# Attention and two expert layers on one core: where three steps of the hand-over to the second expert layer stand in the program

## The chip, the cores and the metric

The kernel runs on one core of a Trainium2 chip, with TensorE (PE), VectorE (DVE), ScalarE (ACT), GpSimd (POOL), SyncE (SP, which here issues DMAs) and the DMA engines. The metric is the device time of one execution in microseconds, as the median of several runs.

## The reference

What is computed, cut to what matters here (4 batches, 8 heads, 576 positions, 64 per head; 2304 tokens of 512; 8 experts with an inner width of 1024):

```python
scores = scale * q @ k.T                       # plus log-decay from f, causal mask
x = softmax(scores) @ v                        # attention; heads side by side: 2304 x 512

def expert_layer(x, logits, w1, w2):           # run twice, with its own weights
    expert_idx = argmax(logits, axis=1)        # one expert for a token
    gate_w = softmax(logits)[range(N), expert_idx]
    for e in range(8):
        mask = expert_idx == e
        h = maximum(x[mask] @ w1[e], 0)        # w1[e]: 512 x 1024
        out[mask] = gate_w[mask, None] * (h @ w2[e])   # w2[e]: 1024 x 512
# layer 1: logits = normed(x) @ normed(expert_emb).T / tau
# layer 2: logits = x @ w_gate, x being what layer 1 gave
```

## The kernel before, in words

The program is one long list of instructions for each engine, in an order written out by hand: each engine works down its list and waits on semaphores where data of another engine is needed. Matrices are kept as a high and a low part, so every product is three matmuls (high by high, high by low, low by high), all recorded at line 1169.

**An expert.** The tokens of one expert are gathered as rows of a DRAM table (`gather`, line 512: an indirect DMA that POOL issues, one for each 128 tokens), turned into columns on PE (`xtrans`, line 520) and split into parts `xh` on ACT (line 523) and `xl` on DVE (line 524). Then come eight W1 steps (`w1_step`, m = 0 to 7, 12 matmuls each; ACT writes `hh`, line 1186, DVE writes `hl`, line 1187) and four W2 groups (`w2_step`, d = 0 to 3, 24 matmuls each for up to 512 tokens, PSUM into `yt`). Weights arrive as chunks `raw` of 512 KB through four buffers; a split (`wts.splits_to`: ACT line 482, DVE line 483) makes the two parts `w`, and the load of a later chunk waits for the split that frees its buffer. A layer takes its experts by rank, fullest first; rank r of layer 1 has room for `CAPS1[r]` tokens, here 256 for the last three, rank 0 of layer 2 for 560.

**The routing of layer 2** is worked out while layer 1 ends. For each finished expert of layer 1 a chain of small links follows: `hot` (which expert a token wants: six DVE instructions, lines 217 to 223), `places` (counts on PE, lines 229 to 253), `leading` (line 323 and on: which expert of layer 2 will be rank 0; from here its weights may be loaded), `slots` (seven DVE instructions, lines 268 to 284, with one each on ACT, line 280, and POOL, line 281), `sums` (matmuls at line 295 and an addition at line 303), and for the last but one expert also `rows` (the index list `idxl2e`, lines 338 to 414, and two gathers of the first 256 tokens of layer 2's rank 0 into `rows`) and `early_columns_2` (those rows into columns `x0h`, `x0l`).

For the last but one expert the string `LATE` says behind which step of the last expert a link stands: a letter and a number, 0 to 7 a W1 step, 8 to 11 a W2 group (h hot, p places, l leading, s slots, u sums, r rows, c early columns).

**The hand-over.** The string `TURN2` then lists what stands between the two layers. The letters: `L` routing products of the last expert's tokens (16 matmuls of 8 columns, line 1269), `R` its output rows (8 transposes, line 1299, and stores to the table), `H`, `P`, `S` its hot, places and sums, `G` the index list `idxl` and three gathers `xg`, the rest of rank 0; `m`k the W1 step k of layer 2's rank 0 on its first 256 tokens and `e`k its ACT and DVE part; `w68` a split; `x`t turns gathered tile t (2, 3, 4) into columns. `I` is `general_1`: a branch (line 1577) around the code for tokens that found no room; with these inputs the branch is taken and its body, hundreds of instructions on PE, is jumped over. `O` is `order_2`: ten DVE instructions (lines 348 to 420) that put the other seven experts of layer 2 in order and give the index list `idxb` of their tokens.

`L2.run` goes on from there. It first gathers the rank 1 tokens (from `idxb`), then does the rest of rank 0's W1 steps, on tokens 256 to 559, 304 columns (called m0' to m7' in this text), then W2; the columns of rank 1 are made behind the first W2 group.

Of the kernel before, what the change touches and what calls it, by code (L numbers as in the profile page):

```python
# [19 lines left out]
P = 128  # L20
NE = 8
# [13 lines left out]
RAWS, RING, LOOK = 4, 6, 4  # L35
FIRST, EARLY = 1, 256
TURN1 = "w2 w3 m0 m1 P e0 m2 e1 w4 m3 S e2 G m4 e3 m5 e4 O m6 e5 x2 m7 e6 e7"
LATE = "h4 p5 l5 s7 u8 r8 c11"
TURN2 = "L R m0 H P e0 m1 m2 e1 S G m4 w68 m3 m6 m5 e3 e2 e6 e4 x2 e5 x3 m7 e7 x4 I O"

PRO = (
# [29 lines left out]
def kernel(  # L71
# [16 lines left out]
    B, H, S, D = q.shape  # L88
# [51 lines left out]
    capr = [const.tile([P, NE], F32, name=f"capr{i}") for i in range(2)]  # L140
# [193 lines left out]
    def pick_lead(sp, acc, fb, Q, name):  # L334
# [6 lines left out]
        )  # L341
        nc.vector.tensor_reduce(ids, x, axis=AX.X, op=ALU.add)
        return ids
# [159 lines left out]
    wts = Weights(wr, wp)  # L503
# [23 lines left out]
    with ExitStack() as actx:  # L527
        p3 = actx.enter_context(tc.tile_pool(name="a3", bufs=3))
# [389 lines left out]
        tots, keys = {-1: None}, {}  # L918
# [180 lines left out]
    class Layer:  # L1099
        def __init__(self, first, pools, weights, src, caps, base):  # L1100
            self.first, self.wts, self.src, self.caps, self.base = first, weights, src, caps, base
            self.sp, self.xp, self.hp, self.yp, self.pp, self.pt, self.pq = pools
            self.cw = P if first else YC
            self.lo = KC * self.cw
            self.w0 = 0 if first else 64
            self.xg, self.nm, self.gt, self.scatters, self.h0, self.x, self.early, self.late = {}, {}, {}, [], None, None, {}, []

        def gather(self, t, ids):
            g = self.xp.tile([P, XW2], F32, tag="xg", name="xg")
# [240 lines left out]
        def early_again(self):  # L1350
            for t in list(self.late):
                self.lead_columns(t)
            for m in list(self.early):
                self.early_mm(m)
                self.early_relu(m)

        def lead_rows(self, idx):

            self.xg[0] = rows0 + [self.gather(t, idx[:, t : t + 1]) for t in range(len(rows0), self.tiles(0))]

        def run(self, idx, idf, pad, after_rank, side):
            caps, wts, w0 = self.caps, self.wts, self.w0
            self.idx, self.idf, self.pad = idx, idf, pad
            yt = None
            for r in range(NE):
                C, b = caps[r], w0 + r * 8
                if r + 1 < NE:
                    self.start_gather(r + 1)
                later = {}
                Hh = self.new_h() if r else self.h0  # L1370
                spans = self.spans(C)
                if r == 0:
                    X = self.x
                    for m in range(FC):
                        self.w1_step(m, wts.ws[b + m // 2], slice(EARLY, C), X, Hh)
                        if m == 2:
                            self.nm[0] = self.norms(self.xg[0])
                        if m == 5:
                            self.start_gates(0)
                        if m % 2:  # L1380
                            wts.splits_to(b + RING - 2 + m // 2)
                else:
                    for m in range(FC):
                        wts.splits_to(min(b + m // 2 + LOOK, w0 + 64))
                        for sl in spans:
                            self.w1_step(m, wts.ws[b + m // 2], sl, X, Hh)
                        if 1 <= m <= self.tiles(r - 1):
                            self.out_step(r - 1, yt, m - 1)
                            if m == self.tiles(r - 1):
                                later = after_rank(r - 1)  # L1390
                        for fn in later.get(m, ()):
                            fn()
                        if self.first and m == 5:
                            self.start_gates(r)
                if not self.first and r == NE - 1:
                    wts.splits_to(w0 + 64)
                    self.last_rows(r, [wts.ws[b + 4 + c] for c in range(4)], Hh)
                    break
                yt = self.new_y()
                for d in range(KC):  # L1400
                    wts.splits_to(min(b + 4 + d + LOOK, w0 + 64 + 4 * self.first))
                    self.w2_step(d, wts.ws[b + 4 + d], C, Hh, yt)
                    for fn in later.get(FC + d, ()):
                        fn()
                    next(side, None)
                    if r + 1 < NE:
                        nt = self.tiles(r + 1)
                        if d == 0:
                            X = self.new_x()
                        for t in [[(0,), (1,), (2,), ()], [(0,), (1, 2), (3, 4), ()]][nt > 3][d]:  # L1410
                            if t < nt:
                                self.xtrans(t, self.xg[r + 1], caps[r + 1], X)
                        if d == 1:
                            self.nm[r + 1] = self.norms(self.xg[r + 1])
                            if not self.first:
                                self.start_gates(r + 1)
            self.yt = yt
# [55 lines left out]
    with ExitStack() as mctx:  # L1473
        sp = mctx.enter_context(tc.tile_pool(name="sp", bufs=1))
# [10 lines left out]
        key2 = sp.tile([P, NE], F32, name="key2")  # L1485
# [3 lines left out]
        def after1(r):  # L1489
# [32 lines left out]
            todo = {}  # L1522
            for u in (LATE if r == NE - 2 else "h4 p6 s7 u10").split():
                todo.setdefault(int(u[1:]), []).append(steps[u[0]])
# [19 lines left out]
        L1 = Layer(True, pools, wts, x_dram, CAPS1, BASE1)  # L1544
        L2 = Layer(False, pools, wts, y_dram, CAPS2, BASE2)
        got = {}
# [16 lines left out]
            TURN1,  # L1563
        )
        (idx1, idf1), pad1, (_, hot1) = got["idx"], got["pad"], got["hot"]
        L1.run(idx1, idf1, pad1, after1, general(sp, keys[B - 1], hot1, capr[0], True))


        last = after1(NE - 1)
# [5 lines left out]
        def general_1():  # L1575
            bg, cap, ci, anew = gen[True]
            with tc.If(nv1 > 0):  # L1577
                go = general_tokens(sp, oh1, pos1, cap, T1)
                ids = assign(sp, pq, "pl", T1, go, pos1, bg, tp1f, "g")
                idxg, idfg = to_index(sp, ids, NC1, N, "g")  # L1580
                padg = to_pad(sp, ids, idfg, NC1, "g")
                kept = [wts.raws[i] for i in range(wts.nsplit, wts.nsplit + RAWS)]
                L1.loop(ci, idxg, idfg, padg, kept, L2.x, x0, L2.h0)
                pm = sp.tile([P, 24], F32, name="pm")
                nc.vector.tensor_tensor(pm, pad1, capmask, op=ALU.max)
                nc.vector.tensor_scalar(pm, pm, anew, None, op0=ALU.add)
                nc.vector.tensor_tensor(padg[:, 0:24], padg[:, 0:24], pm, op=ALU.min)
                route_a(rp, logit2, padg, oh2, NC1)
                route_b(pq, "pl", oh2, pos2, None, NC1, "g", key2)
                for t in range(0, NC1, 5):  # L1590
                    cols = slice(t, min(t + 5, NC1))
                    n = cols.stop - t
                    hots = place_a(rp, pos2[:, cols, :], oh2[:, cols, :], tp2[:, cols], n, Q2)
                    place_b(pq, "pl", *hots, n, Q2, acc2, t == 0, "g")
                nc.vector.tensor_copy(got["l2"], lead_index("l3"))
                L2.early_rows(got["l2"], NC1 * P)
                for t in range(len(rows0), L2.tiles(0)):
                    gather_rows(y_dram, L2.xg[0][t], got["l2"][:, t : t + 1])
                for i, raw in enumerate(kept):
                    wts.load_chunk(wts.nsplit + i, raw)  # L1600
                early_columns_2()
                L2.early_again()

        def order_2():
            sig2, hot2 = got["hot"] = order(sp, key2, lead2[0][1])
            wts.known(1, sig2, range(1, NE))
            ids = by_rank(sp, acc2, hot2, Q2)
            got["idx"] = to_index(sp, ids, 8 * Q2, NC1 * P, "b")
            got["pad"] = to_pad(sp, ids, got["idx"][1], 8 * Q2, "b")
# [4 lines left out]
            {  # L1614
                "m": L2.early_mm, "e": L2.early_relu, "x": L2.lead_columns, "L": lambda: L1.last_logits(L1.yt, NE - 1), "H": last[0],
                "R": lambda: L1.out_last(NE - 1, L1.yt), "P": last[1], "S": last[2], "G": lead_index_2,
                "I": general_1, "O": order_2,
            },
            TURN2,
        )  # L1620
        (idx2, idf2), pad2, (_, hot2) = got["idx"], got["pad"], got["hot"]
        L2.run(idx2, idf2, pad2, lambda r: {}, general(sp, key2, hot2, capr[1], False))
        bg, cap, ci, _ = gen[False]
        nv2 = L2.tile_count(ci)
        with tc.If(nv2 > 0):
# [35 lines left out]
```

## Time and profile before

| | |
|---|---|
| median of 3 runs | 825.51 us (818.5 to 826.73) |
| the profiled execution: own time | 827.05 us |
| its span, first to last instruction | 825.3 us |
| PE busy (matmul) | 778.5 us, 94% |
| PE weight load busy | 739.0 us, 90% |
| DVE, ACT, POOL busy | 545.7, 474.1, 237.2 us |
| mean granted TensorE clock | 0.967 |

Times inside the profile count from the start of the span. Attention ends and layer 1 begins near 270 us; the hand-over to layer 2 lies between some 531 and 592 us. A busy PE is not PE at its peak: at the lower of its two clocks it is as busy and does half.

### The profile page before, as it was taken

What the parts mean: (1) busy time and instruction counts of PE and PEld (TensorE: products, weight loads), DVE (VectorE), ACT (ScalarE), POOL (GpSimd) and SP (SyncE); (2) the same over time, 40 slices, a digit from 0 to 9 for tenths busy, and PEclk for the clock granted to TensorE, in tenths of its full rate; (3) what the DMA queues carried; (4) which work ended last, traced back from release to release, by engine and by line L of the source; (5) the groups of instructions that cost most, each with busy time, mean ns of one, the idle gap of its engine ahead of it and who ended that gap; (6) DMA issues with size and microseconds to landing.
All of it is one profiled execution on the core that took longest, in us unless ns stands there. A gap on an engine that the chain in (4) does not pass through costs nothing. (4 is left out here: it accounts for less than half of the span.)

```text
span 825.3 us, 16797 instructions
## 1 busy us (share of the span) xinstructions
PE 778.5 (94%) x5863; PEld 739.0 (90%) x5863; DVE 545.7 (66%) x1510; ACT 474.1 (57%) x1095; POOL 237.2 (29%) x450
## 2 busy tenths in 40 slices
PE   5999999999999889999999999978899999999995
PEld 4788888988988889999999999968899999999994
DVE  3688887888888834767666777754464556666661
ACT  4788777777778425464565565533343455565650
POOL 5653443543524330321311320112121230122000
PEclk9999999999999957999999999988899999999998
DMA  5858756556663324636646656562244456668740
GB/s 129 203 134 229 187 142 175 138 139 152 164 184 94 98 78 128 202 107 192 195 145 188 193 166 193 162 195 97 83 154 142 151 184 198 197 214 236 205 139 15
DMA packets 201261, 130.51 MB, mean 158 GB/s; under 512 B 85098, under 2 KB 188522, under 8 KB 201167
## 3 DMA queue, kind: packets, MB, share of 16 engines
q1 hardware_dynamic: 195439, 112.47, 48.2%
q0 software_dynamic: 5200, 16.83, 6.1%
q8 instruction: 51, 0.84, 0.4%
q14 instruction: 43, 0.35, 0.1%
q10 hardware_dynamic: 528, 0.02, 0.0%
HBM read 112.05 MB, written 17.75 MB: 157 GB/s over the span
## 5 line engine op out<-in xcount | busy, mean ns | idle before, releaser
L1169 PE MATMUL ps<-xh,w 128*128 128x256 f32 (+8 forms) x1024 | 226.5, 308 | 3.5 <-PEq L1577 2.2
L1169 PE MATMUL ps<-hh,w 128*128 128x256 f32 (+7 forms) x1024 | 218.8, 301 | 0.0
L483 DVE TENSOR_TENSOR w<-raw,w 128x1024 fp32r<-128x1024 f32 x124 | 151.5, 1224 | 56.4 <-ACT w L482 55.8
L1169 PEld LDWEIGHTS ps<-xh,w 128*128 128x128 f32 x1024 | 176.6, 199 | 5.0 <-issue 4.5
L1169 PEld LDWEIGHTS ps<-hh,w 128*128 128x128 f32 x1024 | 168.7, 189 | 1.1 <-ACT hh L1186 0.2
L1169 PE MATMUL ps<-xl,w 128*128 128x256 f32 (+8 forms) x512 | 155.7, 304 | 0.0
L1169 PE MATMUL ps<-hl,w 128*128 128x256 f32 (+7 forms) x512 | 153.1, 299 | 1.4 <-DVE hl L1187 1.3
L1186 ACT ACTIVATE hh<-ps 128x256 fp32r<-128x256 f32 (+8 forms) x144 | 56.1, 397 | 148.8 <-PE ps L1169 146.2
L482 ACT ACTIVATE w<-raw 128x1024 fp32r<-128x1024 f32 x128 | 132.9, 1053 | 0.0
L1187 DVE SCALAR_TENSOR_TENSOR hl<-ps,hh 128x256 fp32r<-128x256 f32 (+8 forms) x144 | 62.8, 441 | 62.7 <-ACT hh L1186 61.5
L1169 PEld LDWEIGHTS ps<-xl,w 128*128 128x128 f32 x512 | 101.9, 199 | 0.2
L1169 PEld LDWEIGHTS ps<-hl,w 128*128 128x128 f32 x512 | 96.9, 189 | 2.9 <-DVE hl L1187 2.5
L745 DVE CUSTOM_DVE_ANT_0 sp<-pS,cum 128x512 f32<-128x512 f32 (+3 forms) x128 | 61.1, 486 | 26.9 <-PE pS L738 25.4
L756 ACT ACTIVATE pm<-sp,sm 128x512 f32<-128x512 f32 (+3 forms) x128 | 71.2, 558 | 4.4 <-DVE sm L745 3.2
L1237 POOL DMA_INDIRECT out_dram<-y,tok x23 | 23.1, 1005 | 175.4 <-ACT y L1233 138.7
L820 DVE TENSOR_TENSOR ptl<-pT,pth 128x128 fp32r<-128x128 f32 (+3 forms) x128 | 59.7, 486 | 9.6 <-ACT pth L817 9.5
L817 ACT ACTIVATE pth<-pT 128x128 fp32r<-128x128 f32 (+3 forms) x128 | 53.6, 435 | 10.6 <-PE pT L813 9.3
L813 PE MATMUL pT<-ident,pm 128*128 128x128 f32 x320 | 57.4, 280 | 1.6 <-DVE ptl L820 1.1
L855 PE MATMUL po<-pth,vv 128*128 128x128 f32 (+2 forms) x192 | 55.9, 310 | 0.1
L855 PE MATMUL po<-ptl,vv 128*128 128x128 f32 (+2 forms) x192 | 53.4, 312 | 0.0
L281 POOL TENSOR_TENSOR l_R<-l_R,tp 128x120 bf16<-128x120 bf16 (+1 forms) x12 | 7.4, 616 | 157.7 <-DVE l_R L276 142.5
L680 POOL CAST qn<-q 128x256 fp32r<-128x256 f32 (+1 forms) x62 | 19.5, 314 | 87.2 <-PE pq L693 54.9
(312 smaller groups left out, 1464.5 us busy)
## 6 DMA issues: line engine op xcount, KB each, us to landing
raw<-in_moe_w_dram SPq DMA_DIRECT2D x128, 512.0 KB, 4.3
cum<-cum_dram SPq DMA_DIRECT2D x15, 576.0 KB, 5.2
k<-in_k_dram SPq DMA_DIRECT2D x64, 128.0 KB, 2.8
cumt<-cum_dram SPq DMA_DIRECT2D x32, 144.0 KB, 4.6
y_dram<-y SPq DMA_DIRECT2D x16, 276.5 KB, 3.6
q<-in_q_dram SPq DMA_DIRECT2D x32, 128.0 KB, 2.5
v<-in_v_dram SPq DMA_DIRECT2D x32, 128.0 KB, 3.2
x_dram<-x SPq DMA_DIRECT2D x16, 256.0 KB, 2.4
```

The source lines that it names most:

```text
L482: nc.scalar.activation(hi, raw, AF.Copy)
L483: eng.tensor_tensor(lo, raw, hi.bitcast(F32), op=ALU.subtract)
L745: nc.vector.tensor_tensor_reduce(out=sp[:, :w], in0=st[j, s, "S", i][:, :w], in1=cums[j][0][:, s, :w], scale=1.0, scalar=3.0e38, op0=ALU.a ...
L756: nc.scalar.activation(pm, st[j, s, "s", i][:, :w], AF.Exp, bias=sm[:, i : i + 1], scale=-1.0, accum_out=sm[:, NT + i : NT + i + 1],)
L813: nc.tensor.transpose(pT[:, c * P : (c + 1) * P], pm[:, c * P : (c + 1) * P], ident)
L817: nc.scalar.activation(pview(j, s, "pth", i, i + 1, P), st[j, s, "T", i], AF.Copy)
L820: nc.vector.tensor_tensor(pview(j, s, "ptl", i, i + 1, P), st[j, s, "T", i], pview(j, s, "pth", i, i + 1, P).bitcast(F32), op=ALU.subtract,)
L855: nc.tensor.matmul(po[:, off + a : off + b], lhsT=vv[:, i, :], rhs=t[:, i * PSTR[s] + a : i * PSTR[s] + b], start=(i == 0 and r == 0), sto ...
L1169: nc.tensor.matmul(ps[:, :n], lhsT=l, rhs=r, start=(i == 0), stop=(i == len(steps) - 1))
L1186: nc.scalar.activation(Hh[0][:, m, sl], ps, AF.Relu)
L1187: nc.vector.scalar_tensor_tensor(Hh[1][:, m, sl], ps, 0.0, Hh[0][:, m, sl].bitcast(F32), op0=ALU.max, op1=ALU.subtract)
L1237: dma = nc.gpsimd.indirect_dma_start(out=out, out_offset=bass.IndirectOffsetOnAxis(ap=tok[:n, t : t + 1], axis=0), in_=y[:n, 0:DM], in_off ...
```

## The change

Three things move; nothing is computed that was not computed before.

- `LATE`: six of the seven links of the last but one expert stand one or two steps earlier: hot behind step 2 instead of 4, places 3 instead of 5, leading 4 instead of 5, slots 5 instead of 7, sums and rows behind step 7 instead of the first W2 group. The early columns stay behind the last W2 group.
- `TURN2`: `H` is named ahead of `R`, `m7` ahead of `e5`, `x2` and `x3`, and `I` and `O` are gone from the list.
- `L2.run` is handed `ordered_2`, which does `general_1` and `order_2`, and calls it ahead of step m3' (`at` is 3): m0' to m2' now stand in front of the branch, and the order and the rank 1 gathers behind them. So that the branch's body can repeat them, `early_again` also repeats the steps `behind`. Layer 1 passes `at` 0, which leaves its order as it was.

```diff
-LATE = "h4 p5 l5 s7 u8 r8 c11"
-TURN2 = "L R m0 H P e0 m1 m2 e1 S G m4 w68 m3 m6 m5 e3 e2 e6 e4 x2 e5 x3 m7 e7 x4 I O"
+LATE = "h2 p3 l4 s5 u7 r7 c11"
+TURN2 = "L H R m0 P e0 m1 m2 e1 S G m4 w68 m3 m6 m5 e3 e2 e6 e4 m7 e5 x2 x3 e7 x4"
...
+            for m in range(self.nbehind):
+                self.behind(m)
+
+        def behind(self, m):
+
+            self.w1_step(m, self.wts.ws[self.w0 + m // 2], slice(EARLY, self.caps[0]), self.x, self.h0)
...
-                if r + 1 < NE:
+                if r and r + 1 < NE:
                     self.start_gather(r + 1)
...
                     for m in range(FC):
-                        self.w1_step(m, wts.ws[b + m // 2], slice(EARLY, C), X, Hh)
+                        if m == at:
+                            self.nbehind = m
+                            self.idx, self.idf, self.pad = ordered()
+                            self.start_gather(1)
+                        self.behind(m)
...
-                        if m % 2:
+                        if m % 2 and m >= at:
                             wts.splits_to(b + RING - 2 + m // 2)
...
-                "I": general_1, "O": order_2,
...
+        def ordered_2():
+            general_1()
+            order_2()
+            return *got["idx"], got["pad"]
...
+        L2.run(ordered_2, 3, lambda r: {}, side_2())
```

How it moves instructions, at three places. First DVE during the last expert of layer 1, around the hot of the last but one (`g_mx` to `oh`; `hl` is a W1 step's low part, `w` a split, `key` belongs to places). Before:

```order
L1187 SCALAR_TENSOR_TENSOR hl<-ps,hh 128x256
L483 TENSOR_TENSOR w<-raw,w 128x1024
L1187 SCALAR_TENSOR_TENSOR hl<-ps,hh 128x256
L217 TENSOR_REDUCE g_mx<-logit_98 128x2
L218 TENSOR_TENSOR g_eq<-logit_98,g_mx 128x16
L219 TENSOR_TENSOR g_eq<-g_eq,wdesc 128x16
L220 TENSOR_REDUCE g_mx<-g_eq 128x2
L222 TENSOR_TENSOR g_mx<-g_mx,pada 128x2
L223 TENSOR_TENSOR oh_100<-g_eq,g_mx 128x16
L1187 SCALAR_TENSOR_TENSOR hl<-ps,hh 128x256
L258 SCALAR_TENSOR_TENSOR key_4741<-psb_7824,wdesc 128x8
```

And now, from the last copy of the previous expert's output (`y<-idfa`) on:

```order
L1222 COPY y<-idfa 128x1
L217 TENSOR_REDUCE g_mx<-logit_98 128x2
L218 TENSOR_TENSOR g_eq<-logit_98,g_mx 128x16
L219 TENSOR_TENSOR g_eq<-g_eq,wdesc 128x16
L220 TENSOR_REDUCE g_mx<-g_eq 128x2
L222 TENSOR_TENSOR g_mx<-g_mx,pada 128x2
L223 TENSOR_TENSOR oh_100<-g_eq,g_mx 128x16
L1188 SCALAR_TENSOR_TENSOR hl<-ps,hh 128x256
L258 SCALAR_TENSOR_TENSOR key_4741<-psb_7791,wdesc 128x8
L307 TENSOR_REDUCE g_s<-oh_100 128x8
L312 TENSOR_TENSOR totb_7802<-totb_7502,g_s 128x8
L483 TENSOR_TENSOR w<-raw,w 128x1024
```

Hot now follows directly on the values that it reads; two `hl` and a split that stood in between come behind it. Second, DVE a little later, around the slots (`l_sl` to `l_ol`), the last two `hl` of the last expert and the addition of the sums (`acc`). Before:

```order
L483 TENSOR_TENSOR w<-raw,w 128x1024
L1187 SCALAR_TENSOR_TENSOR hl<-ps,hh 128x256 x2
L268 TENSOR_TENSOR l_sl<-pos_102,oh_100 128x16
L269 TENSOR_REDUCE l_hi<-l_sl 128x2
L270 TENSOR_SCALAR l_hi<-l_hi 128x2
L271 TENSOR_TENSOR l_eq<-colq,l_hi 128x10
L275 SCALAR_TENSOR_TENSOR l_hi<-l_hi 128x2
L276 TENSOR_TENSOR l_R<-oh_100,l_eq 128x2x40
L284 TENSOR_TENSOR l_ol<-niota,l_hi 128x256
L483 TENSOR_TENSOR w<-raw,w 128x1024
L303 TENSOR_TENSOR acc_4742<-acc_4742,idsb_7947 128x40
```

And now, from the end of the slots on (`gate` are the gate weights of the last expert):

```order
L284 TENSOR_TENSOR l_ol<-niota,l_hi 128x256
L1131 TENSOR_REDUCE gate<-xg 128x1 x2
L1135 TENSOR_TENSOR gate<-gate 128x2
L1141 TENSOR_SCALAR gate<-gate 128x2
L1142 RECIPROCAL gate<-gate 128x2
L483 TENSOR_TENSOR w<-raw,w 128x1024
L1188 SCALAR_TENSOR_TENSOR hl<-ps,hh 128x256 x2
L303 TENSOR_TENSOR acc_4742<-acc_4742,idsb_7915 128x40
```

The slots went ahead of the gates and of the last two `hl`, and the split that stood between the slots and the addition went behind it. Third, PE at the end of the hand-over (`xt` are the column transposes, 128x48 those of x4, `x0h` matmuls those of m7). Before, with the first instruction of the branch's body behind the branch:

```order
L520 MATMUL xt<-ident,xg 128x128 x8
L1169 MATMUL ps<-x0h,w 128x256
L1169 MATMUL ps<-x0l,w 128x256
...
L520 MATMUL xt<-ident,xg 128x48 x4
L1577 COMPARE_AND_BRANCH
L404 LDWEIGHTS s_ol
```

And now, where the 304-column matmuls are those of m0' to m2':

```order
L1170 MATMUL ps<-x0h,w 128x256
L520 MATMUL xt<-ident,xg 128x128 x8
L520 MATMUL xt<-ident,xg 128x48 x4
L1170 MATMUL ps<-xh,w 128x304
L1170 MATMUL ps<-xl,w 128x304
...
L1170 MATMUL ps<-xh,w 128x304
L1587 COMPARE_AND_BRANCH
L404 LDWEIGHTS s_ol
```

The 12 matmuls of m7 stand ahead of all transposes, and 36 matmuls stand between the last of these and the branch.

## Rows read from the trace of the kernel before

**Rows 1.** Whom PE waited for, 531 to 600 us: total, times, longest.

```profile
PE xt L520 <- DMA rows<-y_dram,idxl2e: 3.4, 1, 3.4
PE xt L520 <- DMA xg<-y_dram,idxl: 2.7, 2, 1.8
PE ps L1169 <- PEq L1577: 2.2, 1, 2.2
PE psb L229 <- DVE oh L223: 1.3, 1, 1.3
PE ps L1169 <- issue: 1.3, 1, 1.3
PE ps L1169 <- DVE hl L1187: 0.9, 1, 0.9
PE idsb L295 <- ACT l_R L280: 0.8, 1, 0.8
```

**Rows 2.** Busy time by stretch; behind POOL the granted clock, DMA share and GB/s.

```profile
core 0: us, PE busy (x) PEld busy (x) DVE busy (x) ACT busy (x) POOL busy (x), PEclk, DMA share, GB/s
549.50:553.90 4.40, 0.98 (x7) 0.54 (x5) 1.24 (x3) 0.60 (x1) 0.00 (x0) 0.83 0.92 272
553.90:562.40 8.50, 8.49 (x41) 8.40 (x41) 1.72 (x7) 2.16 (x4) 1.59 (x6) 0.50 0.19 68
571.30:575.30 4.00, 1.27 (x11) 0.85 (x9) 0.65 (x2) 0.87 (x2) 0.25 (x1) 1.00 0.63 209
579.50:586.30 6.80, 5.49 (x22) 5.39 (x23) 2.14 (x7) 0.42 (x1) 3.99 (x4) 0.51 0.37 96
586.30:592.00 5.70, 5.70 (x42) 5.70 (x41) 1.63 (x4) 2.22 (x4) 0.00 (x0) 0.98 0.28 90
600.00:810.00 210.00, 210.00 (x1602) 205.86 (x1602) 126.15 (x229) 105.74 (x196) 36.47 (x35) 1.00 0.58 179
```

**Rows 3.** PE in order of time: start, duration, instruction, idle before.

```profile
553.91 1.12 PE L520 MATMUL xt<-ident,rows 128*128 128x128 f32 x4 [3.42 <-DMA rows<-y_dram,idxl2e]
...
565.43 0.27 PE L295 MATMUL idsb<-l_R,l_ol 128*128 128x40 bf16 x4
...
573.32 0.66 PE L520 MATMUL xt<-ident,xg 128*128 128x128 f32 x4 [1.83 <-DMA xg<-y_dram,idxl]
574.88 0.66 PE L520 MATMUL xt<-ident,xg 128*128 128x128 f32 x4 [0.90 <-DMA xg<-y_dram,idxl]
...
576.88 0.45 PE L520 MATMUL xt<-ident,xg 48*128 48x48 f32 x4
579.52 0.45 PE L1169 MATMUL ps<-xh,w 128*128 128x304 f32 x1 [2.19 <-PEq L1577]
```

**Rows 4.** DVE in order of time.

```profile
539.40 0.16 DVE L268 TENSOR_TENSOR l_sl<-pos,oh 128x16 f32<-128x16 f32 x1
...
540.37 0.42 DVE L284 TENSOR_TENSOR l_ol<-niota,l_hi 128x256 bf16<-128x256 f32 x1
...
543.90 0.17 DVE L414 TENSOR_SCALAR idxl2e<-idfl2e 128x5 int32<-128x5 f32 x1
...
577.75 0.35 DVE L524 TENSOR_TENSOR xl<-xt,xh 128x192 fp32r<-128x192 f32 x1
578.54 0.17 DVE L348 TENSOR_TENSOR o_kb<-key,f_fb 128x8 f32<-128x8 f32 x1 [0.44 <-DVEq L1577]
```

**Rows 5.** POOL in order of time.

```profile
544.35 1.88 POOL L512 DMA_INDIRECT rows<-y_dram,idxl2e  x1 [3.39 <-DVE idxl2e L414]
...
581.31 1.00 POOL L512 DMA_INDIRECT xg<-y_dram,idxb  x1 [9.76 <-DVE idfb L420]
```

**Rows 6.** DMA, 574.5 to 582.5 us: GB/s in 40 slices of 0.2 us; an instruction queue.

```profile
GB/s 22 22 22 0 0 0 0 0 0 0 82 0 0 0 0 0 0 0 0 0 41 0 41 0 0 0 0 82 0 0 0 0 0 0 0 0 0 0 0 0
...
q8 instruction: 2, 0.03, 1.4%
```

**Rows 7.** ACT in order of time.

```profile
604.02 0.60 ACT L523 ACTIVATE xh<-xt 128x512 fp32r<-128x512 f32 x1
```

More of the change, by code (lines that the diff above doesn't have):

```diff
@@ L1106, in __init__ @@
             self.xg, self.nm, self.gt, self.scatters, self.h0, self.x, self.early, self.late = {}, {}, {}, [], None, None, {}, []
+            self.nbehind = 0
         def gather(self, t, ids):
@@ L1355, in early_again, with run @@
                 self.early_relu(m)
+            for m in range(self.nbehind):
+                self.behind(m)
+        def behind(self, m):
+            self.w1_step(m, self.wts.ws[self.w0 + m // 2], slice(EARLY, self.caps[0]), self.x, self.h0)
         def lead_rows(self, idx):
             self.xg[0] = rows0 + [self.gather(t, idx[:, t : t + 1]) for t in range(len(rows0), self.tiles(0))]
-        def run(self, idx, idf, pad, after_rank, side):
+        def run(self, ordered, at, after_rank, side):
             caps, wts, w0 = self.caps, self.wts, self.w0
-            self.idx, self.idf, self.pad = idx, idf, pad
             yt = None
@@ L1372, in run @@
                 if r == 0:
-                    X = self.x
                     for m in range(FC):
-                        self.w1_step(m, wts.ws[b + m // 2], slice(EARLY, C), X, Hh)
+                        if m == at:
[3 more added lines that the diff above has]
+                        self.behind(m)
                         if m == 2:
@@ L1565 @@
         (idx1, idf1), pad1, (_, hot1) = got["idx"], got["pad"], got["hot"]
-        L1.run(idx1, idf1, pad1, after1, general(sp, keys[B - 1], hot1, capr[0], True))
+        L1.run(lambda: (idx1, idf1, pad1), 0, after1, general(sp, keys[B - 1], hot1, capr[0], True))
         last = after1(NE - 1)
@@ L1620, with side_2 @@
         )
-        (idx2, idf2), pad2, (_, hot2) = got["idx"], got["pad"], got["hot"]
-        L2.run(idx2, idf2, pad2, lambda r: {}, general(sp, key2, hot2, capr[1], False))
+        def ordered_2():
+            general_1()
+            order_2()
+            return *got["idx"], got["pad"]
+        def side_2():
+            yield from general(sp, key2, got["hot"][1], capr[1], False)
+        L2.run(ordered_2, 3, lambda r: {}, side_2())
         bg, cap, ci, _ = gen[False]
```

## The prediction

> **What bounds the kernel now.** I read the list of PE's waits first, for the stretch that the change touches, then the busy times by stretch with the granted clock, then the engines in order of time at the places named. From 600 to 810 us PE is busy for all of 210.00 us at clock 1.00 [rows 2]: the second layer is bound by PE and nothing else, so whatever is won or lost ahead of 600 us arrives at the end unchanged. From 531 to 600 us PE waits 12.6 us in all, the sum of [rows 1], in four lumps: 3.0 us around the links of the last but one expert (1.3 on `oh`, 0.9 on `hl`, 0.8 on `l_R`), 3.4 us for the gather of the first rows, 2.7 us for the gather of the rest, 3.5 us at the branch (2.2 on PE's own sequencer, then 1.3 for nothing that the profile shows). Behind the second and the last lump the clock is at its lower level, 1.2 GHz: 0.50 from 553.90 to 562.40 and 0.51 from 579.50 to 586.30 [rows 2]. Work takes twice as long there, so the two cost 8.5/2 = 4.25 us and, without the 1.3 us wait inside, (6.8 - 1.3)/2 = 2.75 us. In front of the first drop PE had 0.98 us of work in 4.40; in front of the second it stood still for 2.19 us [rows 3] after a thin stretch. The wait of 1.83 us at 573.32 [rows 3] was not followed by one: 571.30 to 575.30 is at 1.00 with 1.27 us busy in 4.00 [rows 2]. All told 19.6 us lie here; the question is how much of them the new order sets free.
>
> **Part 1: the links (`LATE`).** The same instructions run on the same engines, so only waits change. Hot can't start before the routing values of the expert's second tile are copied; in the new order it stands right behind that copy, and places still follows one W1 step later. PE will therefore wait on `oh` about as before (1.3 us, bounds 0 and 1.5). Slots now precede the last two `hl` on DVE: they take 1.4 us, from 539.40 to 540.79 [rows 4], and the second W2 product needs those `hl`, for which PE already waits 0.9 us [rows 1]. I take the sum of the three waits, 3.0 us, as unchanged (bounds 2 and 4). What the links do bring is an earlier index list. Before, it was written at 544.07 [rows 4] (start 543.90) and POOL issued the gather at 544.35 [rows 5]; slots ended at 540.79, and a split and five small instructions lay between. Now the additions follow the last `hl` with no split ahead. Just behind these `hl`, the slots began at 539.40; with 1.4 us for the slots put ahead of them and some 1.1 us for the five instructions (a fifth of a microsecond each), the list would be there at 541.9 if DVE got through its queue no sooner, and at about 541.0 if it does, since hot starts two W1 steps earlier. I take 541.5, 2.6 us earlier. The gather's rows, which landed at 553.9, then land near 551.3. Bounds: 549.5, where PE arrives and nothing is left to gain, and 553.9, if the weight loads that share the engines (DMA share 0.92 from 549.50 to 553.90 [rows 2]) set the landing and not the issue.
>
> From those rows to the sums on PE took 553.91 to 565.43, 11.5 us [rows 3], of which 8.5 at the lower clock; at the full one that is 11.5 - 4.25 = 7.3 us. Will the clock hold? The wait shrinks from 3.4 to some 1.8 us, the size of the one at 573.32 that it survived; but the 16 routing products of 8 columns follow directly, thin work where that wait was followed by full steps. I count half of the loss, 2.1 us: sums at 551.3 + 7.3 + 2.1 = 560.7 instead of 565.4, **4.7 us earlier**. Bounds: 0 with a late landing, 8.8 with the earliest and a clock that holds.
>
> `H` ahead of `R` moves nothing: `R` and m0 have no DVE instruction, and hot is DVE's alone, so its place in DVE's row is what it was. Cost nothing, on either side. Leading one step earlier lets SP issue the first two weight loads of layer 2 some 1 us sooner; they are not waited for in [rows 1], and cost nothing.
>
> **Part 2: m7 ahead of x2 and x3, m0' to m2' ahead of the branch.** I count from the sums on (S = 565.43 [rows 3]). The gathers `xg` follow from the sums by a chain that is not touched, so x2 and x3 come at S + 7.9 and S + 9.45 as before. m7, 12 matmuls, fills most of the 1.83 us ahead of x2 instead of standing between x3 and x4. What is late next is x4's data: it lies between x3's landing and 576.88, where x4 ran without waiting; I take 575.5, S + 10.1, as it was gathered 1.3 us behind x3 and the link was idle by 575.1 [rows 6]. From x4's transposes to the end of its low part took 576.88 to 578.10, 1.2 us [rows 3, 4]; with the parts of x3 and m7 queued ahead on ACT and DVE I allow 2.0 us. m0' then starts at S + 12.1 (bounds 11.3 and 13.3) instead of 579.52, S + 14.1. Before, the 36 matmuls of m0' to m2' ended near S + 22.8: 22 of them by 586.3, 14 more at 0.136 us (5.70/42 [rows 2]). Now they take 36 x 0.136 = 4.9 us plus what the clock costs. The stretch from m7's end to m0' is thin (12 transposes in nearly 5 us), so I expect the drop again, a little earlier relative to m0': 2.1 us instead of 2.75 (bounds 0 and 3.4).
>
> The branch now lies behind 36 matmuls. In [rows 6] the two larger bars are the fetches of PE's queue q8, 16 KB each; the first is at 576.5 to 576.7, ahead of x4's own transposes (576.88). So the sequencer had reached the branch while the array was still at m7, and PE stood until 579.52, some 3 us behind the fetch, because just four transposes lay between. With 4.9 us of matmuls ahead and a sequencer that runs ahead, the fetch is **covered**; the cover missing altogether would cost the 3.5 us of before. DVE paid 0.44 us at its branch [rows 4], and pays it again.
>
> The Trainium skill (Runtime: NRT & Kernel Launch, Instruction fetch mechanics) says that a taken branch whose target is outside the two pages held forces a fetch of the target page before execution can go on; the trace agrees, with the two fetches and the waits of 2.2 and 1.3 us beside them. By that rule alone a branch amid the matmuls stops PE just as it did in front of them, and the sum would be 3.5 us smaller: it is rival 2.
>
> The order's ten instructions, 578.54 to 581.3, 2.8 us [rows 4, 5], stood where DVE had nothing else; now they stand between the `hl` of m2' and m3'. Behind them on DVE are m3' to m5' `hl`, a split and the gates, for which PE waits at the first W2 group at the latest. DVE is busy 1.63 of 5.70 us there [rows 2], so this is nearly all covered; I charge 0.5 us (bounds 0 and 2.8). m3' starts at S + 12.1 + 4.9 + 2.1 + 0.5 = S + 19.6 instead of S + 22.8: **3.2 us earlier** (bounds -1 and 5.5).
>
> POOL's gathers for rank 1 now wait for an order behind m2': issued some 4.3 us after m3' starts at most, where they were issued at 581.31, 7 us ahead of it. They are needed when the first W2 group is over, 604.02 [rows 7], 15.5 us after m3' started: 11 us are left for a landing. The nearest landing is that of `rows`, issued at 544.35 [rows 5] with the second of the pair in at 553.9, 9.6 us under heavy load. Covered, with little to spare. SP's loads for rank 1 wait for the order too, but for a split behind m3' in any case.
>
> **Sum.** 4.7 + 3.2 = 7.9 us. The profiled execution took 827.05 us and would take 819.2; it lies 1.5 us above the median of 825.51, so against the median: **817.6 us**.
>
> **Rivals.** (1) The first gather lands no earlier, since the DMA share of 0.92 and not its issue sets it: then only part 2 is left, 825.5 - 3.2 = 822.3. For it: the share; against it: POOL waited 3.39 us for the index list right ahead of the issue [rows 5]. (2) The branch isn't covered: PE stands 3.5 us amid m3', part 2 gives -0.3, and 825.5 - 4.4 = 821.1. Against it: the early fetch of [rows 6]. (3) Both drops of the clock go away: 7.3 + 5.3 = 12.6 us, 813. For it: the waits that the clock survived; against it: two thin stretches stay. (4) Slower: the late order. If rank 1's first rows need more than 11 us to land, PE waits for every further microsecond, and behind a wait like that of 3.4 us it works at the lower clock, 4 us more as after 553.9. At a landing of 14.8 us (3.8 + 4.1 = 7.9) nothing is left of the gain; at 23 us the kernel takes 825.5 - 7.9 + 12 + 4 = 834. Against it: the 9.6 us is the longest near by. That the change does less than it says is true of `H` alone.
>
> **How the numbers follow.** Forecast 58%, rival 1 12%, rival 2 10%, rival 3 15%, rival 4 5%. One per cent, about what a measurement of this kernel can tell from no change, is 8.3 us: 817.3 is the line, and the forecast sits just short of it. Of its 58 points 28 lie beyond the line, with the better landing or clock, and 30 short. With rival 3, faster by over 1%: 0.43. Rivals 1 and 2 and the rest of the forecast are within 1%: 0.52. Rival 4: 0.05. For eight in ten the range takes in rivals 1 and 2 and the earliest landing with one drop left: 812 to 823.5.
>
> **What the changed profile would show.** Part 1 is right if the gather of `rows` issues near 541.7, PE's wait for it is 1 to 2 us, and the sums stand near 560 us. Part 2 is right if PE has no wait at the branch, m7 lies ahead of x2, and the clock still falls around m0'. The forecast is wrong if the wait for `rows` stays over 3 us, if a wait on PE's sequencer appears behind m2', if PE waits on `hl` for longer than 3 us at the first W2 group of layer 2, or if a transpose of rank 1 waits for its gather.

## The result and the profile after

| | before | after |
|---|---|---|
| median | 825.07 us (11 runs, 818.5 to 826.73) | 815.17 us (11 runs, 812.73 to 816.96) |
| ratio to the kernel before, 95% interval | | 0.9893 [0.9872, 0.9913] |
| profiled execution, own time | 827.05 us | 815.17 us |
| its span | 825.3 us | 813.5 us |
| mean granted TensorE clock | 0.967 | 0.973 |

The median fell by 9.9 us, where 7.9 were forecast (817.6 us). By the ratio, which isn't the quotient of the two medians, the gain is 8.8 us (7.2 to 10.6). Whom PE waited for in the hand-over, 531 to 600 us, in the changed kernel (total, times, longest), beside [rows 1]:

```profile
PE ps L1170 <- PEq L1587: 1.4, 1, 1.4
PE xt L520 <- DMA xg<-y_dram,idxl: 1.0, 2, 0.8
PE ps L1170 <- DVE hl L1188: 0.9, 1, 0.9
PE ps L1170 <- ACT xh L523: 0.7, 1, 0.7
PE idsb L295 <- DVE gate L1131: 0.5, 1, 0.5
```

The wait for `rows`, 3.4 us before, is gone, and so is the 1.3 us "issue" wait at the branch. The wait on PE's own sequencer (PEq) has shrunk from 2.2 to 1.4 us but stands in a new place. Hot's wait on `oh` now lies ahead of this stretch (1.07 us, ended at 528.73). New is a wait of 0.7 us for `xh` in front of m0'. The busy times by stretch, beside [rows 2]:

```profile
core 0: us, PE busy (x) PEld busy (x) DVE busy (x) ACT busy (x) POOL busy (x), PEclk, DMA share, GB/s
548.40:556.60 8.20, 8.20 (x76) 7.79 (x75) 4.91 (x19) 4.22 (x10) 1.96 (x7) 1.00 0.62 186
556.60:592.15 35.55, 31.81 (x228) 30.35 (x227) 18.31 (x54) 13.54 (x35) 12.58 (x10) 0.95 0.39 124
568.60:572.00 3.40, 3.40 (x14) 3.40 (x15) 0.02 (x1) 0.42 (x1) 0.00 (x0) 0.50 0.00 0
600.00:798.00 198.00, 198.00 (x1506) 193.91 (x1506) 119.22 (x215) 101.97 (x188) 33.88 (x32) 1.00 0.55 174
```

From the transposes of `rows` to the sums PE is now busy throughout at clock 1.00; before, most of that path ran at 0.50. Of the second drop 3.40 us at 0.50 are left, in m0' and m1'. The second layer is as full as before, so nothing is given back there. PE in order of time, beside [rows 3]:

```profile
548.40 1.12 PE L520 MATMUL xt<-ident,rows 128*128 128x128 f32 x8
549.51 1.92 PE L1270 MATMUL pg<-wg,yt 128*128 128x8 f32 x16
556.60 0.27 PE L295 MATMUL idsb<-l_R,l_ol 128*128 128x40 bf16 x4
564.36 0.66 PE L520 MATMUL xt<-ident,xg 128*128 128x128 f32 x4 [0.28 <-DMA xg<-y_dram,idxl]
565.78 1.15 PE L520 MATMUL xt<-ident,xg 128*128 128x128 f32 x8 [0.76 <-DMA xg<-y_dram,idxl]
567.62 0.41 PE L1170 MATMUL ps<-xh,w 128*128 128x304 f32 x1 [0.69 <-ACT xh L523]
568.44 0.52 PE L1170 MATMUL ps<-xl,w 128*128 128x304 f32 x1 [0.41 <-DVE xl L524]
576.54 0.38 PE L1170 MATMUL ps<-xh,w 128*128 128x304 f32 x1 [1.45 <-PEq L1587]
```

x3 and x4 are one row of 8 transposes here; m0' starts at 567.62, and m3' at 576.54 behind the wait at the branch. DVE, beside [rows 4] (the first row is the copy behind which hot stands, which I use as the start of the count; the `hl` is that of m3'):

```profile
527.35 0.15 DVE L1222 COPY y<-idfa 128x1 f32<-128x1 f32 x1
533.72 0.16 DVE L268 TENSOR_TENSOR l_sl<-pos,oh 128x16 f32<-128x16 f32 x1
540.33 0.17 DVE L414 TENSOR_SCALAR idxl2e<-idfl2e 128x5 int32<-128x5 f32 x1
576.39 0.17 DVE L348 TENSOR_TENSOR o_kb<-key,f_fb 128x8 f32<-128x8 f32 x1 [0.34 <-DVEq L1587]
579.02 0.47 DVE L1188 SCALAR_TENSOR_TENSOR hl<-ps,hh 128x304 fp32r<-128x304 f32 x1
```

POOL and ACT, beside [rows 5] and [rows 7]:

```profile
540.79 1.88 POOL L512 DMA_INDIRECT rows<-y_dram,idxl2e  x1 [5.44 <-DVE idxl2e L414]
579.16 1.00 POOL L512 DMA_INDIRECT xg<-y_dram,idxb  x1 [16.43 <-DVE idfb L420]
592.15 0.60 ACT L523 ACTIVATE xh<-xt 128x512 fp32r<-128x512 f32 x1
```

The same copy in the kernel before:

```profile
528.04 0.15 DVE L1221 COPY y<-idfa 128x1 f32<-128x1 f32 x1
```

These rows cut the gain into three. Ahead of the copy the profiled execution after is 0.69 us earlier, with nothing changed there. From the copy to the sums it took 565.43 - 528.04 = 37.39 us and takes 29.25: 8.1 us. From the sums to the first `xh` of rank 1 it took 604.02 - 565.43 = 38.59 us and takes 35.55: 3.0 us. Together 11.9 us, the difference of the two profiled executions (827.05 - 815.17). That is 2 us more than the medians differ by, since the profiled execution of before was 2 us above its median.

### The profile page after: what moved, and what is told of

Same layout as the page of the kernel before. It is cut to its first block, busy times and chain, and to the rows that moved or that the text cites. A ratio compares the mean times of both kernels' runs of the same rounds, so it can differ in the third digit from the quotient of the medians.

```text
span 813.5 us, 16798 instructions
## 1 busy us (share of the span) xinstructions
PE 774.7 (95%) x5863; PEld 735.2 (90%) x5863; DVE 545.0 (67%) x1510; ACT 474.7 (58%) x1095; POOL 238.3 (29%) x450
## 5 line engine op out<-in xcount | busy, mean ns | idle before, releaser
L680 POOL CAST qn<-q 128x256 fp32r<-128x256 f32 (+1 forms) x62 | 19.6, 317 | 88.5 <-PE pq L693 55.8
```

## The experiments

**The theory**: two levers act one after the other, the issue time of the first gather (links) and the place of the branch; each is worth what it takes from PE's waits plus the work done at the lower clock behind them. **The rivals**: for the links, that the landing is set by the traffic and not by the issue; for the second half, that m7's place or the order's place does it and not the branch; for the late order, that it uses up the room of the rank 1 gathers.

All runs in one table; times in us. Medians are of 12 runs at most and 4 at least (e4_branch_only 4, e7_no_branch and e9_branch_at_x2 6, e5_sums_late 7); ratios are to the kernel before in the same batch (its median there 824.71 to 825.07) and are not the quotients of the medians: the two differ most in e2_no_links, 5.0 us of gain by the ratio and 3.3 by the medians. The other columns are of each one's profiled execution, which is up to 3.0 us slower than its median (822.25 for 819.21 in e10_branch_old_place), so they don't add up to the medians. They are read from its rows in order of time: the first gather's issue and the sums counted from the start of that copy, PE's wait for `rows`, the granted clock from the last row of transposes of `rows` to the sums, and the time from the sums to the first `xh` of rank 1. In the last column "ahead" and "behind" say where the branch stands, ahead of m0' or behind m2'.

| kernel | median | ratio, interval | issue | wait | clock | sums | sums to `xh` |
|---|---|---|---|---|---|---|---|
| before | 825.07 | | 16.31 | 3.42 | 0.62 | 37.39 | 38.59 ahead |
| after | 815.17 | 0.9893 [0.9872, 0.9913] | 13.44 | 0 | 1.00 | 29.25 | 35.55 behind |
| e1_links_only | 819.11 | 0.9938 [0.9914, 0.9962] | 13.45 | 0.69 | 0.69 | 33.22 | 38.42 ahead |
| e2_no_links | 821.42 | 0.9939 [0.9909, 0.9969] | 16.30 | 2.69 | 0.69 | 36.16 | 33.82 behind |
| e3_m7_only | 818.21 | 0.9915 [0.9885, 0.9946] | 13.44 | 0.35 | 1.00 | 29.75 | 38.34 ahead |
| e4_branch_only | 815.56 | 0.9890 [0.9841, 0.9939] | 13.45 | 0.17 | 0.82 | 31.26 | 37.22 behind |
| e5_sums_late | 819.73 | 0.9926 [0.9890, 0.9961] | 14.57 | 2.29 | 0.58 | 36.67 | 35.73 behind |
| e6_gather_late | 823.04 | 0.9972 [0.9949, 0.9995] | 17.27 | 2.72 | 0.60 | 36.90 | 36.70 behind |
| e7_no_branch | 815.71 | 0.9888 [0.9859, 0.9918] | 13.43 | 1.39 | 0.68 | 33.77 | 33.53 none |
| e9_branch_at_x2 | 816.29 | 0.9901 [0.9875, 0.9928] | 13.44 | 0.32 | 1.00 | 29.71 | 37.69 at x2 |
| e10_branch_old_place | 819.21 | 0.9933 [0.9909, 0.9957] | 13.44 | 0.80 | 0.69 | 33.07 | 38.92 ahead |
| e8_at5 | 818.90 | 0.9945 [0.9917, 0.9973] | 13.44 | 0.84 | 0.82 | 31.49 | 39.33 behind m4' |

**The halves apart.** Four kernels: the links alone; all but the links; links and m7 with the branch ahead of m0'; links and branch with m7 at its old place.

```diff
 # e1_links_only: new LATE, and
-        L2.run(ordered_2, 3, lambda r: {}, side_2())
+        L2.run(ordered_2, 0, lambda r: {}, side_2())
+TURN2 = "L R m0 H P e0 m1 m2 e1 S G m4 w68 m3 m6 m5 e3 e2 e6 e4 x2 e5 x3 m7 e7 x4"
 # e2_no_links: the change, but
+LATE = "h4 p5 l5 s7 u8 r8 c11"
 # e3_m7_only: the change, but at is 0
 # e4_branch_only: the change, but TURN2 as in e1_links_only
```

> New LATE alone; TURN2's order and the place of branch and order as in the kernel before. Theory A (the earlier index list lets the first gather land before PE gets there, so the wait of 3.4 us goes and the clock never falls at that place): 817 us, 8 us less than before; no wait on the gather of rows, the sums about 8 us earlier, the stall of 2.2 + 1.3 us at the branch and the drop of the clock behind it still there. Rival B (the links only bring the wait, and the clock falls at the routing products all the same): 821 to 822 us, with the granted clock at 0.50 for several us behind 549 us. Rival C (the gain is that of the later branch and the links only fill a wait that comes back): 824 to 825 us.

> The change without the new LATE: m7 ahead of x2 and x3, and branch and order behind m2'. Theory A: the wait of some 3.4 us for the gather of rows and the clock at 0.50 behind it stay, only the part behind the sums is gained: 822 us, 3 us less than before. Rival B: 820 to 821 us. Rival C: 816 us, nearly all of the gain.

> The changed kernel with branch and order back ahead of m0' (new LATE and new TURN2 kept). Theory A: the branch comes at once behind x4 again, PE stands 2 us or more for the fetch there, some of it while the parts of x4 are made, and m7 fills the wait ahead of x2: 816 to 817.5 us, 1 to 2 us more than the changed kernel. If m7's new place were the whole gain of part 2 (rival): 815 us, as the changed kernel. If it brings nothing: 818 us, as with the links alone.

> The changed kernel with m7 back between x3 and x4 (branch and order behind m2' kept). Theory A: PE waits about 1.8 us ahead of x2 again, and x4 follows m7 1.4 us later than its data: 816.0 to 816.8 us, about 1 us more than the changed kernel. If m7's new place were the whole gain of part 2: 818 us. If it brings nothing: 815 us.

By the ratios the links alone give 0.62% or 5.1 us (interval 3.1 to 7.1), the rest alone 0.61% or 5.0 us (2.6 to 7.5), both 1.07% or 8.8 us (7.2 to 10.6): they add up within the intervals. With m7's place old and all else new (e4_branch_only) the ratio is 0.9890, near that of the change, but from 4 runs, with an interval of 4 us to either side: it can't tell what m7's place adds. In the traces m0' starts 13.51 us after the sums there (557.93 to 571.44) and 11.0 to 11.4 us after them in the four others with the branch behind m2'. The path to `xh` is 1.7 us longer than the change's, but nearly all of this is the lower clock (mean clocks of 0.91 and 0.95 over the path), so what the earlier m0' is worth at the end isn't shown. With the branch ahead of m0', m7's place is worth 0.9938 - 0.9915, 1.9 us, with intervals that overlap, and in the traces m0' starts as late with it (14.11 us after the sums in e3_m7_only) as without it (13.99 in e1_links_only). The last column sorts by the branch: ahead of m0' 38.59, 38.42, 38.34 and 38.92; behind m2' 35.55, 33.82, 37.22, 35.73 and 36.70, a mean of 35.8 to one of 38.6. Not all of these 2.8 us is waiting: over the same stretch the mean granted clock is 0.91, 0.91, 0.91 and 0.87 with the branch ahead, and 0.95, 1.00, 0.91, 0.95 and 0.91 with it behind, so that some 1.8 us of the difference goes to the lower clock (an estimate, the share missing from 1.00 times the length). Whether the branch's place sets that clock isn't shown: the change and e2_no_links, which have the same order from the sums on, stand at 0.95 and 1.00.

**The issue of the first gather.** The links stay early up to the slots; sums and rows go behind the first W2 group (e5_sums_late), or rows behind the second (e6_gather_late).

```diff
-LATE = "h2 p3 l4 s5 u7 r7 c11"
+LATE = "h2 p3 l4 s5 u8 r8 c11"    # e5_sums_late
+LATE = "h2 p3 l4 s5 u8 r9 c11"    # e6_gather_late
```

> The changed kernel with sums and rows of the last but one expert behind the first W2 group again (u8 r8), hot to slots early as in the change. Theory A (what counts of the links is when the first gather is issued): the index list comes 1 to 2.5 us later than in the changed kernel, PE waits 0.5 to 2 us for the rows, 816 to 818 us. Rival D (it is the earlier hot, places and leading that count, by the waits on DVE that they spare): 815 us, as the changed kernel.

> As the run with sums late, but rows behind the second W2 group (u8 r9): the first gather is issued later than in the kernel before. Theory A: PE waits 3 us or more for the rows, the clock is at 0.50 behind it for 7 to 10 us, 821 to 824 us. Rival D: 815 to 817 us.

e6_gather_late in order of time on POOL and PE:

```profile
544.28 1.88 POOL L512 DMA_INDIRECT rows<-y_dram,idxl2e  x1 [9.26 <-DMA raw<-in_moe_w_dram]
551.13 1.97 PE L520 MATMUL xt<-ident,rows 128*128 128x128 f32 x8 [2.72 <-DMA rows<-y_dram,idxl2e]
```

And the busy times of the stretch behind, in the columns of before:

```profile
551.13:563.91 12.78, 12.78 (x75) 12.61 (x75) 4.65 (x18) 4.68 (x10) 1.97 (x7) 0.60 0.18 64
```

A gather 3.8 us later (17.27 for 13.44) takes back 0.79% of the 1.07%, 6.5 us, and brings back the wait of 2.72 us and the clock of 0.60. This answers the first rival: the issue is the lever. The price may be steep from the start: in e5_sums_late 1.13 us of delay cost 0.33%, 2.7 us, but with intervals that overlap, so it isn't shown; in its profiled execution PE waits 2.29 us and works at 0.58 behind it, while its seven runs range from 813.33 to 823.31.

**The branch by itself.** Left out, put ahead of x2, and put back ahead of m0' with the order left behind m2'. In e9_branch_at_x2 `I` stands for the branch, and `e7` moves ahead of it. e7_no_branch leaves out the code for tokens without room, which these inputs never run, and the branch with it.

```diff
 # e7_no_branch, and e9 and e10 as well: ordered_2 without it
         def ordered_2():
-            general_1()
             order_2()
 # e9_branch_at_x2 and e10_branch_old_place: TURN2 ends
+"... m7 e5 e7 I x2 x3 x4"
+"... m7 e5 x2 x3 e7 x4 I"
```

> The changed kernel without the branch of the first layer's general path: it leaves out the code for tokens that found no room in layer 1, which these inputs never run. It prices the branch amid the steps. Theory A (the jump costs what PE waited on its sequencer there, 1.4 us, and DVE's 0.3 us is hidden): 813.5 us, 1.5 us less than the changed kernel. Rival E (the branch is covered by the 36 matmuls in most runs, and the 1.4 us is what the order on DVE would cost anyway): 815 us.

> The changed kernel with the branch alone ahead of x2 (behind m7 and its parts), where PE waits for the gather in any case; the order stays behind m2'. Theory A (the jump costs about 3 us from the instruction at which PE's sequencer meets it, and hides under a wait): x2 starts up to 2 us later than its data, x4 is bound by its landing, no wait at m3': 814 to 815 us, 0 to 1 us less than the changed kernel. Rival (the jump empties PE at any place and the clock falls behind it): 816 to 817 us.

> The changed kernel, with the branch alone put back to its old place, behind x4 and in front of m0'; the order and the rank 1 gathers stay behind m2'. Theory A, that the 3 us of part 2 come from taking PE's sequencer away from the place where only four transposes cover it: PE waits 2 to 4 us on its sequencer in front of m0', and the time is 2 to 4 us above the changed kernel, 817 to 819 us. Theory B, that they come from taking the order's DVE work and its wait out of the way of m0': the time stays at 815 to 816 us.

PE's waits in e10_branch_old_place, 515 to 625 us:

```profile
PE ps L1170 <- PEq L1587: 3.8, 1, 3.8
PE xt L520 <- DMA xg<-y_dram,idxl: 1.2, 2, 1.0
PE psb L229 <- DVE oh L223: 1.1, 1, 1.1
PE ps L1170 <- issue: 1.1, 1, 1.1
```

With only the branch put back, 0.40% or 3.3 us of the gain go (0.9933 for 0.9893, with intervals that just touch), and PE again stands on its sequencer, 3.8 us, and on "issue", 1.1 us. The order, late in that kernel too, gives nothing by itself that the intervals could show: it stands at 0.9933 where e3_m7_only, with the order early, has 0.9915. So it is the branch, by the traces and, at the edge of the intervals, by the times. Without any branch the ratio is that of the change, 0.9888 to 0.9893; the path from the sums on is 2.0 us shorter in its trace (33.53 for 35.55), which the intervals, some 0.2 to 0.3% to either side, can't resolve. But PE's list there has no wait at all at m3', with the order in its place behind m2': the 1.45 us of the change is the branch's and not the order's.

Ahead of x2, behind the steps m4 to m7, which PE works through without a wait, it stood longest of all:

```profile
569.48 2.53 PE L520 MATMUL xt<-ident,xg 128*128 128x128 f32 x12 [4.01 <-PEq L1587]
```

About 1 us of this it would have waited for `xg` anyway (1.0 in the change). The path was 2.1 us longer; the ratio, 0.9901, isn't told apart either.

**A later order.** Branch, order and rank 1 gathers behind m4'; the two splits that belong to m1' and m3' then come only behind m5', since `run` splits only from m = `at` on (in the change the one of m1' already stands behind m3').

```diff
-        L2.run(ordered_2, 3, lambda r: {}, side_2())
+        L2.run(ordered_2, 5, lambda r: {}, side_2())
```

> The changed kernel, with the branch, the order and the rank 1 gathers behind m4' instead of m2'. Theory A, that the late order has room to spare at the changed kernel's place: the gathers issue some 4 us later, near 583, are still in before rank 1's transposes near 591, and the time is within 1 us of the changed kernel, 814.5 to 816.5 us. Theory B (rival 4), that the room was nearly used up: PE waits for the rank 1 gather 1 to 5 us and works at the lower clock behind it, 818 to 823 us.

PE's waits, 515 to 625 us:

```profile
PE xt L520 <- DMA xg<-y_dram,idxl: 1.6, 2, 0.8
PE ps L1170 <- DVE o_kb L348: 1.5, 1, 1.5
PE ps L1170 <- issue: 1.3, 1, 1.3
...
PE ps L1170 <- ACT w L482: 0.9, 1, 0.9
...
PE ps L1170 <- DVE w L483: 0.7, 1, 0.7
```

The first gather for rank 1 on POOL and its transposes on PE, in order of time:

```profile
582.84 1.00 POOL L512 DMA_INDIRECT xg<-y_dram,idxb  x1 [20.32 <-DVE idfb L420]
595.09 0.60 PE L520 MATMUL xt<-ident,xg 128*128 128x128 f32 x4
```

By the ratios it is 4.3 us slower than the change (0.9945 for 0.9893), so my first theory's time (814.5 to 816.5) failed; but not in rival 4's way: the gathers, issued at 582.84, are turned at 595.09 without a wait. By its trace PE waited for the splits that came late, 0.9 and 0.7 us in the first W2 group, and at the branch twice, 1.5 (put down to `o_kb`, the first instruction behind DVE's branch) and 1.3 us. Against the change the path from the sums is 3.8 us longer: 1.7 of splits, 1.3 more at the branch (2.8 for 1.45), 0.6 more for `xg`.

## Why the prediction was right, and where it was not

**What bounds the kernel.** Right: what was won ahead of 600 us arrived at the end (11.9 us on the path, 11.88 in the execution's time).

**Part 1, the mechanism right, its size put too small for the profiled run.** I had 4.7 us; the trace has 8.1. Three terms: the index list was there at 540.50, not 541.5, of which 0.69 is the earlier start; PE reached the transposes at 548.40 and not at 549.5, and `rows` was in, where I had a landing at 551.3 and a wait of 1 to 2 us; so the clock held, where I charged half of 4.25 us. Every kernel with the new `LATE` issues at 13.4 after the copy, and yet its sums come anywhere from 29.25 to 33.77, with a wait of 0 to 1.39 us and a clock of 1.00 to 0.68 behind it, though up to the sums all eight run the same instructions. The mean of those eight is 31.4, against 36.8 of before and e2_no_links: 5.3 us, and 5.1 us by the ratio of the links alone. "Half of the clock loss" was right on average, not as what one execution does: some executions keep the clock, others lose most of it, and that this one kept it is luck. The waits of the links themselves, 3.0 us unchanged, measured 1.07 + 0.94 + 0.51 = 2.5. `H` ahead of `R` shows nowhere, but was not run alone.

**Part 2, the sum right, the cover wrong.** 3.2 us forecast, 3.0 in the trace, and m3' at S + 19.94 for S + 19.6 (S the start of the sums; before, it was S + 23.1, where I had 22.8). The failed step is "the fetch is covered": a wait on PE's sequencer behind m2', which I had named as a sign against the forecast, is there, 1.45 us. The fetches of PE's instructions after, 570 to 578 us in 40 slices of 0.2 us, beside [rows 6]:

```profile
GB/s 0 0 0 0 0 0 0 0 0 0 0 0 0 0 0 0 0 82 0 0 0 0 0 0 0 0 0 0 0 0 0 0 41 123 0 0 0 0 0 0
...
q8 instruction: 2, 0.03, 1.9%
```

The first 82 is PE's fetch, near 573.5; PE goes on at 576.54, 3.0 us later, as it did before (576.6 to 579.52). But it shows just 1.5 us before the last matmul of m2' was through (576.54 - 1.45 = 575.09). If the fetch goes out as soon as the sequencer meets the branch, which no run shows, the sequencer was not 36 matmuls ahead but only some 11 (1.5 us at 0.136); in any case no more than that much of the 3 us was hidden. By the Trainium skill (Runtime: NRT & Kernel Launch, Instruction fetch mechanics), a taken branch to a page that isn't held stops the engine until the page is fetched; the trace agrees that it stops, and the price in this trace is the 3.0 us less what is queued. The sum still came out, by errors that cancel, since other terms were too dear: x4 came at once behind x3 and m0' at S + 11.02 (I had 12.1, at least 11.3), and the lower clock lasted 3.40 us, a loss of 1.7 (I had 2.1). The order on DVE, charged 0.5, cost nothing on PE: the `hl` of m3' followed it at 579.02, and no wait for it is in the list. e10_branch_old_place shows that the branch's place carries this part. m7's place I had counted as a way to an earlier m0': the traces bear that out (S + 13.51 with m7 at its old place, S + 11.02 in the change), but what it is worth at the end isn't shown.

**The rivals.** (1), a landing that the issue doesn't set, falls with e6_gather_late. (2), a branch that isn't covered, is half true, 1.45 of 3.5 us. (3), both drops gone, came half true in this execution: the first gone, the second smaller. (4), the late order, falls: rank 1's gathers, issued at 579.16, were in by 591.5, and even at 582.84 nothing waited. What makes a later order slow, by the trace of e8_at5, is the branch and the splits tied to it.

**What stays open.** Behind each taken branch a second fetch follows, and 1 to 2 us after PE went on it stops a second time with the branch ahead of m0' (1.3 us of "issue" before, 2.1 in e1_links_only, 1.6 in e3_m7_only, 1.1 in e10_branch_old_place) and behind m4' (1.3), but in no kernel with the branch behind m2' or ahead of x2. That the fetch makes the stop isn't shown. Which instructions come in with the branch's target may do this; it wasn't tried. Nor is it known why PE stood 4.0 us in e9_branch_at_x2, behind dense work.

## What to carry over

Taking away PE's wait for a gather can be worth more than the wait: behind a wait of 2.72 us the work from the transposes to the sums took 12.78 us, most of it at the lower clock, where 8.20 do. A taken branch here cost PE some 3 us from fetch to work in ten of eleven traces, and what PE still had to do hid at most 1.9 us of it. Dense work ahead of a branch helps only as far as the fetch goes out early, so look for the fetch in the trace; and move what hangs on the branch only as far as nothing else is held up with it.

## What the runs showed of the hardware

- With the same issue time (13.4 us after the copy) the second tile of `rows` was waited for until 21.8 us after it in e4_branch_only and until 23.0 in e7_no_branch: the landing varies by 1.2 us and more between executions, and with the clock behind it the sums vary by 4.5 us (29.25 to 33.77).
- The clock fell behind waits as short as 0.17 us (0.82 in e4_branch_only) and 0.69 us (0.69 in e1_links_only), and held behind 0.32 and 0.35 us (1.00 in e9_branch_at_x2 and e3_m7_only). The wait's length alone doesn't decide it. The 16 routing products of 8 columns follow in all of them, and PE counts as busy through them (1.00 of each 1.00 us from 549 to 554 in e4_branch_only, where the clock is down to 0.51 from 551).
- After a taken branch PE went on 2.9, 3.0 and 3.3 us behind its fetch in before, after and e10_branch_old_place, with 4 transposes, 36 matmuls and 8 transposes ahead of it, and likewise 2.8 to 3.3 us in seven more. e9_branch_at_x2 is the exception: PE's fetches show at 564.7 and 564.9 us, amid 200 to 410 GB/s of other traffic where the ten had next to none, and PE went on at 569.48, 4.6 us behind the later one. That the traffic is the reason isn't shown.
- PE's stop at the branch was 1.25 to 1.58 us in the six kernels with 36 or more matmuls of the steps m0' on ahead of it; in the five with the branch further ahead it was 1.2 us (e1_links_only), 2.2 (before), 3.7, 3.8 and 4.0 (e9_branch_at_x2). The traces put these stops down to PE's sequencer, to DVE's or to `o_kb`.
